# Turning keys and queries two tiles at a time, as 4-byte pairs of channels, in a fused agent-attention and maxout kernel

## The chip, the cores and the metric

The kernel runs on one core of a Trainium2 chip as one launch. The metric is the device time of one execution in microseconds: 256.32 us is the median of three runs (254.13 to 256.45). A profile of one further execution (254.07 us) gives the lines quoted here.

The core has five engines with instruction streams of their own: PE (TensorE: weight loads and matmuls, a turn of a tile among them), ACT (ScalarE), DVE (VectorE), POOL (GpSimd) and SP (SyncE, which issues the transfers here). SBUF is the working memory; PE writes to the eight banks of PSUM, and ACT and DVE copy from there.

## The reference

```python
q, k, v: (4, 12544, 128);  agents: (4, 49, 128);  w1, w2, w3: (128, 768);  w_out: (768, 128)

def sm(a, b):
    s = scale * (a @ b.transpose(0, 2, 1))
    s = s - s.max(-1, keepdims=True)
    e = np.exp(s)
    return e / (e.sum(-1, keepdims=True) + 1e-09)
a2k = sm(agents, k)
agent_v = a2k @ v
q2a = sm(q, agents)
x = (q2a @ agent_v).reshape(50176, 128)
h = np.maximum(np.maximum(x @ w1, x @ w2), x @ w3)
out = h @ w_out
```

All inputs and the output are float32. Inside, the kernel computes on bf16 values with float32 sums.

## The kernel before, in words

Tokens are handled in tiles of 128 on the partitions, with their 128 channels along the row. Each of the four batches has 98 tiles.

**Keys and values.** The 98 key tiles of a batch are 14 groups of KT = 7. Loads bring four groups at a time (28 tiles, 1792 KB for keys and as much for values; the first load of the first batch brings two groups) into five large SBUF buffers, LD. For group `kB.G` the steps are, by name: `kc` casts the keys to bf16 on POOL (into KB), `kt` turns each tile on PE so that channels are on the partitions (line L314, with the bf16 identity as the moving operand), `ke` copies the turned group from PSUM to KT on DVE (L320), `ks` multiplies each turned tile with the 49 agents of the batch (agT, L325), `kx` takes the exponent on ACT (into EK, where each tile has 64 columns, 49 of them used), `vc` casts the values (into VB, with two columns of ones behind the 128), and `kv` sums exponent times value over the batch (L339). In `kv` two tiles share a product: their 128 exponent columns are the weights and 2 x 130 value columns move, and the blocks on the diagonal are used afterwards. The seventh tile of a group is alone: 64 weight columns and 130 moving ones.

**From agents to a linear map.** After the 14 groups of a batch the sums are normalised and multiplied with the differences of the three weight matrices. Hidden units for which one of the three is largest for all agents are folded into a linear map; the others, up to 64, get a place in two small matrices. All that goes into a table G per batch. A test at the end takes a general and slow path where there are more than 64 such units; its code is not run on this data.

**Queries.** 49 query groups `s` of GT = 8 tiles: `qc` cast on POOL (QB), `qt` turn on PE (L314), `qe` copy on ACT (L568, into QT), `sc` scores, `ex` exponent on ACT (EQ), `su` and `re` sums and their reciprocals, `u`, `v`, `a`, `x` the hidden units, `p` the output products, `ov` scaling on DVE, and `st` the store of three groups at a time. In `sc` the scores of even tiles go to the lower 64 partitions of a PSUM bank and those of odd tiles to the upper 64, by two products with 64 weight columns each and 512 moving ones (L574).

**What sets the order.** The order of all steps, and the buffer and PSUM bank of each, stand in a table in the file, written out step by step; the kernel only emits it. Each engine works through its own steps in that order. A load is issued on SP when the buffer's last reader, a cast, is done. The first step, `prep` (L284), turns the agents and lays them out as agT; its turned agents stand in PSUM bank 0, which the first key turn needs next.

Of the kernel before, what the change touches and what calls it, by code (L numbers as in the profile page):

```python
# [9 lines left out]
FP32 = mybir.dt.float32  # L10
BF16 = mybir.dt.bfloat16
# [13 lines left out]
VC = C + 2  # L25
# [9 lines left out]
SLOTS = {"M": 8, "LD": 5, "QB": 3, "KB": 3, "VB": 4, "KT": 3, "QT": 3, "EQ": 8, "EK": 4, "AS": 3, "R": 3, "OS": 5}  # L35
SHAPE = {"LD": ([P, max(TK * KT, LONG), C], FP32), "QB": ([P, GT, C], BF16), "KB": ([P, KT, C], BF16), "VB": ([P, KT, VC], BF16),
         "KT": ([P, KT * C], BF16), "QT": ([P, GT, P], BF16), "EQ": ([P, 512], BF16), "EK": ([P, KT * H], BF16),
         "AS": ([P, 512], BF16), "R": ([P, 512], BF16), "OS": ([P, LONG, C], FP32)}
# [49 lines left out]


def mm(n, cols):  # L90
    t = n * max(cols / 2400 + 0.0025, 0.0253)
    return t, t + 0.235
# [18 lines left out]
def graph(plan, em):  # L111
    add = plan.add
    add("prep", PE, em.prep, (0.5, 4.0))
    for b in range(B):
        for g in range(NCH):
# [5 lines left out]
            add(f"kc{r}", POOL, em.cast("k", "kb", b, g, POOL), pool(KT * C), after=[f"kl{z}"], new=[("KB", f"kb{r}")], use=[f"k{z}"])  # L121
            add(f"kt{r}", PE, em.k_turn(r), mm(KT, 128), after=[f"kc{r}", "prep"], new=[("M", f"kT_ps{r}")], use=[f"kb{r}"])
            add(f"ke{r}", DVE, em.k_evacuate(r), (0.53, 0.72), after=[f"kt{r}"], new=[("KT", f"kT{r}")], use=[f"kT_ps{r}"])
            add(f"ks{r}", PE, em.k_scores(b, r), mm(KT, 49), after=[f"ke{r}"], new=[("M", f"s{r}")], use=[f"kT{r}"])
            add(f"kx{r}", ACT, em.k_exps(r), (0.34, 0.5), after=[f"ks{r}"], new=[("EK", f"e{r}")], use=[f"s{r}"])
            eng = ACT if b == 0 else POOL
# [72 lines left out]
class Emit:  # L199
    def __init__(self, tc, pools, io):  # L200
# [12 lines left out]
        self.sums_of = const.tile([P, KEYS + NQ * GT], FP32, name="sums_of")  # L213
        self.ag_st, self.ag_bf = self.slots["OS"][-1][:AP_, :A // 7, :], self.slots["QT"][-1][:AP_, :A // 7, :]
        nc.scalar.dma_start(self.ag_st, io["agents"].rearrange("b a c -> (b a) c").rearrange("(p j) c -> p j c", p=AP_))
# [8 lines left out]
        nc.vector.memset(self.agT, 0.0)  # L224
        self.sel = const.tile([P, 2], BF16, name="sel")
# [58 lines left out]
    def prep(self):  # L284
        nc = self.nc
        nc.vector.tensor_copy(out=self.ag_bf, in_=self.ag_st)
        t, u = self.psum[:, 0, :].bitcast(BF16), self.psum[:, 1, :]
        t = t[:, :A // 7 * 32].rearrange("c (j x) -> c j x", x=32)[:, :, :AP_]
        for j in range(A // 7):
            nc.tensor.transpose(t[:, j, :], self.ag_bf[:, j, :], self.ident[:AP_, :AP_])  # L290
        self.mul(u[:, :H], self.ones, self.earlier[:, 1:1 + H], True)
        nc.vector.tensor_copy(out=self.agT[:, :, :A].rearrange("c b (q j) -> c j b q", j=A // 7), in_=t.rearrange("c j (b q) -> c j b q", b=B))
        nc.vector.tensor_copy(out=self.slot_of, in_=u[:, :H])
# [8 lines left out]
    def cast(self, which, to, b, g, eng):  # L302
        def fn():
            z = load_of(b, g)[0]
            out, src = self.t[f"{to}{b}.{g}"][:, :, :C], self.t[f"{which}{b}.{z}"][:, (g - z) * KT:(g - z + 1) * KT, :]
            if eng == ACT:
                self.nc.scalar.activation(out, src, AF.Copy)  # L307
            else:
                self.nc.gpsimd.tensor_copy(out=out, in_=src)  # L309
        return fn  # L310
# [4 lines left out]

    def k_turn(self, r):
        return lambda: self.turn(self.t[f"kT_ps{r}"].bitcast(BF16), self.t[f"kb{r}"], KT)

    def k_evacuate(self, r):
        return lambda: self.nc.vector.tensor_copy(out=self.t[f"kT{r}"], in_=self.t[f"kT_ps{r}"].bitcast(BF16)[:, :KT * C])  # L320

    def k_scores(self, b, r):
# [5 lines left out]
    def k_exps(self, r):  # L328
        def fn():
            e, s = self.t[f"e{r}"].rearrange("p (j h) -> p j h", h=H), self.t[f"s{r}"][:, :KT * A].rearrange("p (j a) -> p j a", a=A)  # L330
            self.nc.scalar.activation(e[:, :, :A], s, AF.Exp, scale=SCALE)  # L331
# [232 lines left out]
    def q_turn(self, s):  # L564
        return lambda: self.turn(self.t[f"qT_ps.{s}"].bitcast(BF16), self.t[f"qb.{s}"], GT)

    def q_evacuate(self, s):
        return lambda: self.nc.scalar.activation(self.t[f"qT.{s}"].rearrange("p j c -> p (j c)"), self.t[f"qT_ps.{s}"].bitcast(BF16),  # L568
                                                 AF.Copy)
# [55 lines left out]

    def in_general(self):
        self.keys_in_general()
        self.queries_in_general()

    def keys_in_general(self):  # L630

        nc, ps, slots = self.nc, self.psum, self.slots
        kf, vf, kb, vb, kT, e = (slots[cls][i] for cls, i in (("LD", 0), ("LD", 1), ("KB", 0), ("VB", 0), ("KT", 0), ("EK", 0)))
        vb, e = vb[:, :, :C], e[:, :KT * A]
        eT = slots["QT"][0].rearrange("p j c -> p (j c)")[:A, :KT * P]
# [6 lines left out]
        def scores(b, g):  # L642
            nc.gpsimd.dma_start(kf[:, :KT, :], rows("k", b, g))
            nc.gpsimd.tensor_copy(out=kb, in_=kf[:, :KT, :])
# [30 lines left out]
    def queries_in_general(self):  # L675
# [13 lines left out]
        for s in range(NQ):  # L689
# [5 lines left out]
            nc.gpsimd.dma_start(self.near(s, q, GT), self.far("q", s, GT))  # L695
            nc.gpsimd.tensor_copy(out=qb, in_=q[:, half, :])
            self.turn(ps[:, 6, :].bitcast(BF16), qb, GT)
# [168 lines left out]
```

## Time and profile before

| what | before |
|---|---|
| median of three runs | 256.32 us (254.13 to 256.45) |
| profiled execution | 254.07 us, its span 252.2 us |
| PE busy | 207.6 us (82%) |
| DVE busy | 167.8 us (67%) |
| POOL busy | 151.1 us (60%) |
| ACT busy | 147.3 us (58%) |
| transfers | 104.91 MB, mean 416 GB/s |
| largest part of the chain of waits | PE, 62% |

The span runs from the first to the last instruction of the profile; the execution's own time has 1.9 us around it. An engine's busy time is the union of its instructions' times. Matmuls overlap one another, so that PE's busy time contains their run-out as well as their issue; where a step from one matmul to the next is wanted, it is worked out from the start times and the length of a merged group.

### The profile page before, as it was taken

What the parts mean: (1) busy time and instruction counts of PE and PEld (TensorE: products, weight loads), DVE (VectorE), ACT (ScalarE), POOL (GpSimd) and SP (SyncE); (2) the same over time, 40 slices, a digit from 0 to 9 for tenths busy, and PEclk for the clock granted to TensorE, in tenths of its full rate; (3) what the DMA queues carried; (4) which work ended last, traced back from release to release, by engine and by line L of the source; (5) the groups of instructions that cost most, each with busy time, mean ns of one, the idle gap of its engine ahead of it and who ended that gap; (6) DMA issues with size and microseconds to landing.
All of it is one profiled execution on the core that took longest, in us unless ns stands there. A gap on an engine that the chain in (4) does not pass through costs nothing.

```text
span 252.2 us, 6372 instructions
## 1 busy us (share of the span) xinstructions
PE 207.6 (82%) x2509; PEld 149.2 (59%) x2509; DVE 167.8 (67%) x357; ACT 147.3 (58%) x240; POOL 151.1 (60%) x171
## 2 busy tenths in 40 slices
PE   0693787759999979989898789998988989999910
PEld 0472654738686657776766567765665656676600
DVE  7342512684686689685857886585758899888940
ACT  2445257217585859285756674666566787777620
POOL 2251751896979476979691599695774444439100
PEclk9999568698999999999999999999999999999985
DMA  6999999999999999999999999999999999999994
GB/s 252 437 425 427 431 428 429 429 422 430 429 422 427 426 433 426 427 425 428 421 431 434 422 434 421 429 430 419 431 426 427 425 424 424 428 424 424 429 417 169
DMA packets 11071, 104.91 MB, mean 416 GB/s; under 512 B 1150, under 2 KB 2174, under 8 KB 3866
## 3 DMA queue, kind: packets, MB, share of 16 engines
q1 hardware_dynamic: 10992, 104.34, 97.9%
q8 instruction: 21, 0.34, 0.5%
q10 hardware_dynamic: 42, 0.10, 0.2%
q14 instruction: 16, 0.13, 0.1%
HBM read 78.74 MB, written 25.69 MB: 414 GB/s over the span
## 4 chain that ended last, share of the span: by engine, by line
PE 62%; DVE 15%; ACT 10%; DMA 5%; issue 4%; POOL 1%; ACTq 0%; DVEq 0%; POOLq 0%
PE psum L282 46%; PE psum L314 15%; DMA LD<-in_k_dram 5%; ACT QT L568 4%; DVE OS L619 3%; ACT EQ L580 2%; DVE KT L320 2%; ACT VB L307 1%; DVE gap L432 1%; DVE R L603 1%; ACT EK L331 1%; POOL KB L309 1%; DVE cand L431 1%; ACT AS L600 1%; DVE open L435 1%
## 5 line engine op out<-in xcount | busy, mean ns | idle before, releaser
L309 POOL CAST KB<-LD 128x896 bf16<-128x896 f32 x56 | 52.5, 969 | 43.7 <-DMA LD<-in_k_dram 26.2
L562 POOL CAST QB<-LD 128x1024 bf16<-128x1024 f32 x49 | 49.8, 1046 | 24.2 <-DMA LD<-in_q_dram 12.2
L619 DVE TENSOR_TENSOR OS<-psum,sums_of 128x512 f32<-128x512 f32 x97 | 61.1, 678 | 4.7 <-PE psum L282 4.5
L568 ACT ACTIVATE QT<-psum 128x1024 bf16<-128x1024 bf16 x49 | 50.3, 1026 | 18.4 <-PE psum L314 17.8
L320 DVE COPY KT<-psum 128x896 bf16<-128x896 bf16 x56 | 34.3, 620 | 24.7 <-PE psum L314 21.3
L282 PE MATMUL psum<-VB,EK 128*128 128x260 bf16 x224 | 40.3, 282 | 4.6 <-ACT VB L307 3.0
L331 ACT ACTIVATE EK<-psum 128x343 bf16<-128x343 f32 x56 | 25.7, 467 | 24.8 <-PE psum L282 14.9
L600 ACT ACTIVATE AS<-psum 128x512 bf16<-128x512 f32 x49 | 29.1, 597 | 17.9 <-PE psum L282 16.1
L314 PE MATMUL psum<-ident,KB 128*128 128x128 bf16 x392 | 35.4, 240 | 4.7 <-POOL KB L309 3.5
L603 DVE TENSOR_TENSOR R<-psum,AS 128x512 bf16<-128x512 f32 x49 | 32.7, 679 | 9.4 <-PE psum L282 4.3
L309 POOL CAST VB<-LD 128x896 bf16<-128x896 f32 x42 | 38.5, 957 | 0.3 <-DMA LD<-in_v_dram 0.3
L580 ACT ACTIVATE EQ<-psum 128x512 bf16<-128x512 f32 x49 | 29.3, 598 | 13.4 <-PE psum L282 12.7
L282 PEld LDWEIGHTS <-EK 128*128 128x128 bf16 x224 | 20.5, 103 | 24.6 <-issue 17.3
L314 PEld LDWEIGHTS <-KB 128*128 128x128 bf16 x392 | 27.5, 108 | 9.0 <-POOL KB L309 4.8
L282 PEld LDWEIGHTS <-EQ 128*128 128x128 bf16 x392 | 25.9, 97 | 10.6 <-ACT EQ L580 5.7
L282 PE MATMUL psum<-EQ,G 128*128 128x512 bf16 (+1 forms) x104 | 31.3, 366 | 0.4 <-DVE OS L619 0.2
L314 PE MATMUL psum<-ident,QB 128*128 128x128 bf16 x392 | 30.6, 222 | 0.1
L282 PE MATMUL psum<-G,R 128*128 128x256 bf16 x196 | 29.4, 273 | 1.3 <-DVE R L603 1.2
L282 PE MATMUL psum<-G,EQ 128*128 128x256 bf16 x196 | 29.4, 272 | 0.0
L314 PEld LDWEIGHTS <-QB 128*128 128x128 bf16 x392 | 23.4, 99 | 7.3 <-issue 5.9
L282 PE MATMUL psum<-QT,agT 128*64 128x512 bf16 (+1 forms) x104 | 20.1, 384 | 5.8 <-ACT QT L568 5.7
L282 PE MATMUL psum<-agT,KT 128*128 128x49 bf16 x392 | 20.7, 191 | 2.4 <-DVE KT L320 2.2
(97 smaller groups left out, 178.5 us busy)
## 6 DMA issues: line engine op xcount, KB each, us to landing
LD<-in_q_dram SPq DMA_DIRECT2D x16, 1536.0 KB, 16.2
out_dram<-OS SPq DMA_DIRECT2D x15, 1536.0 KB, 19.7
LD<-in_k_dram SPq DMA_DIRECT2D x12, 1792.0 KB, 14.3
LD<-in_v_dram SPq DMA_DIRECT2D x12, 1792.0 KB, 15.8
LD<-in_k_dram SPq DMA_DIRECT2D x4, 896.0 KB, 14.3
LD<-in_v_dram SPq DMA_DIRECT2D x4, 896.0 KB, 12.7
LD<-in_moe_w_dram SPq DMA_DIRECT2D x3, 384.0 KB, 12.9
out_dram<-OS SPq DMA_DIRECT2D x2, 512.0 KB, 11.1
```

The source lines that it names most:

```text
L282: self.nc.tensor.matmul(out, w, x, start=start, stop=True, skip_group_check=True)
L307: self.nc.scalar.activation(out, src, AF.Copy)
L309: self.nc.gpsimd.tensor_copy(out=out, in_=src)
L314: self.nc.tensor.transpose(t[:, j * P:(j + 1) * P], src[:, j, :], self.ident)
L320: return lambda: self.nc.vector.tensor_copy(out=self.t[f"kT{r}"], in_=self.t[f"kT_ps{r}"].bitcast(BF16)[:, :KT * C])
L331: self.nc.scalar.activation(e[:, :, :A], s, AF.Exp, scale=SCALE)
L562: return lambda: self.nc.gpsimd.tensor_copy(out=self.t[f"qb.{s}"], in_=self.half("q", s))
L568: return lambda: self.nc.scalar.activation(self.t[f"qT.{s}"].rearrange("p j c -> p (j c)"), self.t[f"qT_ps.{s}"].bitcast(BF16), AF.Copy)
L580: return lambda: self.nc.scalar.activation(self.t[f"e.{s}"], self.t[f"qs.{s}"], AF.Exp, scale=SCALE)
L600: return lambda: self.nc.scalar.activation(self.t[f"a.{s}"], self.t[f"u.{s}"], AF.Relu)
L603: return lambda: self.nc.vector.tensor_tensor(out=self.t[f"r.{s}"], in0=self.t[f"v.{s}"], in1=self.t[f"a.{s}"], op=ALU.max)
L619: self.nc.vector.tensor_tensor(out=out, in0=src, in1=rc.unsqueeze(2).to_broadcast([P, 4, C]), op=ALU.mult)
```

## The change

Two neighbouring tiles of bf16 values are 256 values in a row of SBUF. Seen as float32 they are 128 elements of 4 bytes, each a pair of neighbouring channels. One turn of such a block, with a float32 identity, moves both tiles: partition 64 h + i then holds the pair of channels 2i and 2i + 1 of tile h, one pair per token. So four turns do for eight tiles.

The even channels (parity x = 0) are every second bf16 element of the turned block, the odd ones the rest. The agents are laid out to match, in agP: for each parity, tile h of the pair has its own 64 rows and its own columns, with zeros elsewhere. A product over one parity gives half of the score of both tiles at once; the products of the two parities are summed in PSUM. For keys the weights are a parity of the turned block (every second element) and 2 x 49 agent columns move. For queries the copy from PSUM on ACT sorts the parities apart, and two full products of 128 weight columns and 512 moving ones write all 128 partitions of the bank.

Groups must have an even number of tiles, so key groups alternate between 8 and 6; a load of four groups is still 28 tiles. The table of the order is the same word for word, and so are all transfers. In `prep` the agents' cast, turns and layout are made in more pieces: two casts for one, 14 turns for 7, four copies for one.

```diff
+def tiles_of(g):
+    z = g // 2 * 2 * KT + g % 2 * (KT + 1)
+    return z, KT - 1 if g % 2 else KT + 1
...
-        self.agT = const.tile([P, B, H], BF16, name="agT")
+        self.agP = const.tile([P, 2, B, 2, H], BF16, name="agP")
+        self.ident_of_pairs = const.tile([P, P], FP32, name="ident_of_pairs")
+        nc.vector.tensor_copy(out=self.ident_of_pairs, in_=self.ident)
...
     def prep(self):
-        nc.vector.tensor_copy(out=self.ag_bf, in_=self.ag_st)
+        for h in range(2):
+            nc.vector.tensor_copy(out=self.ag_bf[:, :, :, h, :], in_=self.ag_st.rearrange("p j (i x) -> p j x i", x=2))
...
-        nc.vector.tensor_copy(out=self.agT[:, :, :A].rearrange("c b (q j) -> c j b q", j=A // 7), in_=t.rearrange("c j (b q) -> c j b q", b=B))
+        for h in range(2):
+            r = slice(h * H, (h + 1) * H)
+            for x in range(2):
+                nc.vector.tensor_copy(out=self.agP[r, x, :, h, :A].rearrange("c b (q j) -> c j b q", j=A // 7),
+                                      in_=t[r, x, :, :].rearrange("c j (b q) -> c j b q", b=B))
...
+    def turn_pairs(self, t, src, n):
+        two = src.rearrange("p j c -> p (j c)").bitcast(FP32)
+        for i in range(n // 2):
+            self.nc.tensor.transpose(t[:, i * P:(i + 1) * P], two[:, i * P:(i + 1) * P], self.ident_of_pairs)
...
     def k_scores(self, b, g, r):
-            for j in range(KT):
-                self.mul(self.t[f"s{r}"][:, j * A:(j + 1) * A], self.t[f"kT{r}"][:, j * P:(j + 1) * P], self.agT[:, b, :A], j == 0)
+            kT = self.t[f"kT{r}"].rearrange("p (i n x) -> p i n x", n=P, x=2)
+            for i in range(tiles_of(g)[1] // 2):
+                for x in range(2):
+                    self.mul(self.t[f"s{r}"][:, 2 * i * A:2 * (i + 1) * A], kT[:, i, :, x], self.agP[:, x, b, :, :A], i == 0 and x == 0)
...
     def values(self, b, g):
-            for j in range(0, KT, 2):
-                n = min(2, KT - j)
-                self.mul(acc[:n * H, :n * VC], e[:, j * H:(j + n) * H], vb[:, j:j + n, :].rearrange("p j c -> p (j c)"), g == 0 and j == 0)
+            for j in range(0, tiles_of(g)[1], 2):
+                self.mul(acc[:, :2 * VC], e[:, j * H:(j + 2) * H], vb[:, j:j + 2, :].rearrange("p j c -> p (j c)"), g == 0 and j == 0)
...
     def q_evacuate(self, s):
-        return lambda: self.nc.scalar.activation(self.t[f"qT.{s}"].rearrange("p j c -> p (j c)"), self.t[f"qT_ps.{s}"].bitcast(BF16),
-                                                 AF.Copy)
+        return lambda: self.nc.scalar.activation(self.t[f"qT.{s}"].rearrange("p (x i) n -> p x (i n)", x=2),
+                                                 self.t[f"qT_ps.{s}"].bitcast(BF16).rearrange("p (n x) -> p x n", x=2), AF.Copy)

     def scores(self, s, out, qT):
         for i, (b, _, n, jj, pairs) in enumerate(parts_of(s)):
-            for h in range(2):
-                self.mul(out[h * H:(h + 1) * H, jj * P:(jj + pairs) * P], self.agT[:, b, :], qT[:, h::2, :][:, jj:jj + pairs, :], i == 0)
+            for x in range(2):
+                self.mul(out[:, jj * P:(jj + pairs) * P], self.agP[:, x, b, :, :].rearrange("p h a -> p (h a)"),
+                         qT[:, x * GT // 2 + jj:x * GT // 2 + jj + pairs, :].rearrange("p i n -> p (i n)"), i == 0 and x == 0)
```

What stands on an engine changes at three places on which the prediction rests. The first is PE at the end of the first group's weighted values, `kv0.0`, and the start of the second group's scores, `ks0.1`. EK and KT are buffers of weights, VB and agT (agP) what moves; the size is that of the output. Before:

```order
L282 LDWEIGHTS EK_94
L282 MATMUL psum<-VB_76,EK_94 128x260
L282 LDWEIGHTS EK_94
L282 MATMUL psum<-VB_76,EK_94 64x130
L282 LDWEIGHTS KT_81
L282 MATMUL psum<-agT,KT_81 128x49
```

And after the change:

```order
L291 LDWEIGHTS EK_94
L291 MATMUL psum<-VB_76,EK_94 128x260
L291 LDWEIGHTS EK_94
L291 MATMUL psum<-VB_76,EK_94 128x260
L291 LDWEIGHTS KT_81
L291 MATMUL psum<-agP,KT_81 128x98
```

The product on half of the array is gone, and a score product has 98 columns where it had 49.

The second is PE at the scores of the first query group, `sc.0`, ahead of which stands the last linear product of the first batch, `py0`. Before:

```order
L282 LDWEIGHTS pick
L282 MATMUL psum<-wo_bf,pick 64x128
L282 LDWEIGHTS agT
L282 MATMUL psum<-QT_83,agT 64x512
L282 LDWEIGHTS agT
L282 MATMUL psum<-QT_83,agT 64x512
```

And after:

```order
L291 LDWEIGHTS pick
L291 MATMUL psum<-wo_bf,pick 64x128
L291 LDWEIGHTS agP
L291 MATMUL psum<-QT_83,agP 128x512
L291 LDWEIGHTS agP
L291 MATMUL psum<-QT_83,agP 128x512
```

Two products on 64 partitions each have become two on all 128.

The third is DVE at the start, in `prep` and the first two copies of turned keys. OS and QT are borrowed as staging for the agents. Before:

```order
L286 CAST QT_85<-OS_108 28x896
L292 COPY agT<-psum 128x7x4x7
L293 COPY slot_of<-psum 128x64
L320 COPY KT_80<-psum 128x896
L320 COPY KT_81<-psum 128x896
```

And after:

```order
L296 CAST OS_108<-OS_108 28x14x64 x2
L306 COPY agP<-psum 64x7x4x7 x4
L308 COPY slot_of<-psum 128x64
L344 COPY KT_80<-psum 128x1024
L344 COPY KT_81<-psum 128x768
```

Ahead of the first key copy there are three more copies and one more cast, and the key copies alternate in size.

More of the change, by code (lines that the diff above doesn't have):

```diff
@@ L121, in graph @@
             add(f"kc{r}", POOL, em.cast("k", "kb", b, g, POOL), pool(KT * C), after=[f"kl{z}"], new=[("KB", f"kb{r}")], use=[f"k{z}"])
[L122 to L125, printed above, removed]
+            add(f"kt{r}", PE, em.k_turn(g, r), mm(KT, 128), after=[f"kc{r}", "prep"], new=[("M", f"kT_ps{r}")], use=[f"kb{r}"])
+            add(f"ke{r}", DVE, em.k_evacuate(g, r), (0.53, 0.72), after=[f"kt{r}"], new=[("KT", f"kT{r}")], use=[f"kT_ps{r}"])
+            add(f"ks{r}", PE, em.k_scores(b, g, r), mm(KT, 49), after=[f"ke{r}"], new=[("M", f"s{r}")], use=[f"kT{r}"])
+            add(f"kx{r}", ACT, em.k_exps(g, r), (0.34, 0.5), after=[f"ks{r}"], new=[("EK", f"e{r}")], use=[f"s{r}"])
             eng = ACT if b == 0 else POOL
@@ L222, in __init__ @@
             nc.vector.memset(v[:, :, C:], 1.0)
[L223 to L224 removed]
+        self.agP = const.tile([P, 2, B, 2, H], BF16, name="agP")
+        nc.vector.memset(self.agP, 0.0)
+        self.ident_of_pairs = const.tile([P, P], FP32, name="ident_of_pairs")
+        nc.vector.tensor_copy(out=self.ident_of_pairs, in_=self.ident)
         self.sel = const.tile([P, 2], BF16, name="sel")
@@ L304, in fn @@
             z = load_of(b, g)[0]
-            out, src = self.t[f"{to}{b}.{g}"][:, :, :C], self.t[f"{which}{b}.{z}"][:, (g - z) * KT:(g - z + 1) * KT, :]
+            first, n = tiles_of(g)
+            out, src = self.t[f"{to}{b}.{g}"][:, :n, :C], self.t[f"{which}{b}.{z}"][:, first - z * KT:first - z * KT + n, :]
             if eng == ACT:
@@ L626, in in_general @@
     def in_general(self):
+        self.agT = self.slots["EQ"][-1][:, :B * H].rearrange("p (b h) -> p b h", b=B)
+        for x in range(2):
+            r = slice(x * H, (x + 1) * H)
+            self.nc.vector.tensor_copy(out=self.agT[r, :, :], in_=self.agP[r, x, :, x, :])
         self.keys_in_general()
@@ L643, in scores @@
             nc.gpsimd.dma_start(kf[:, :KT, :], rows("k", b, g))
-            nc.gpsimd.tensor_copy(out=kb, in_=kf[:, :KT, :])
+            nc.gpsimd.tensor_copy(out=kb.rearrange("p j (x i) -> p j x i", x=2), in_=kf[:, :KT, :].rearrange("p j (i x) -> p j x i", x=2))
             self.turn(ps[:, 0, :].bitcast(BF16), kb, KT)
@@ L695, in queries_in_general @@
             nc.gpsimd.dma_start(self.near(s, q, GT), self.far("q", s, GT))
-            nc.gpsimd.tensor_copy(out=qb, in_=q[:, half, :])
+            nc.gpsimd.tensor_copy(out=qb.rearrange("p j (x i) -> p j x i", x=2), in_=q[:, half, :].rearrange("p j (i x) -> p j x i", x=2))
             self.turn(ps[:, 6, :].bitcast(BF16), qb, GT)
```

38 lines of the change are left out of this document (22 added, 16 removed).

## The prediction

> **What bounds the kernel now.** I read the page's shares and slices first, then the table by stretch, then the end of the queue of stores, and last PE's rows one by one, because PE is what the change rewrites.
>
> ```profile
> span 252.2 us, 6372 instructions
> PE 207.6 (82%) x2509; PEld 149.2 (59%) x2509; DVE 167.8 (67%) x357; ACT 147.3 (58%) x240; POOL 151.1 (60%) x171
> DMA packets 11071, 104.91 MB, mean 416 GB/s; under 512 B 1150, under 2 KB 2174, under 8 KB 3866
> ...
> 0.00:6.00 6.00, 0.00 (x0) 0.00 (x0) 4.83 (x29) 1.28 (x1) 1.20 (x9) 1.00 0.68 243
> 6.00:12.00 6.00, 4.11 (x40) 2.93 (x40) 2.28 (x5) 2.58 (x4) 1.75 (x2) 1.00 1.03 441
> ...
> 60.00:200.00 140.00, 130.07 (x1655) 94.61 (x1653) 102.18 (x207) 90.45 (x151) 101.57 (x112) 1.00 1.01 427
> 200.00:240.00 40.00, 37.35 (x423) 25.19 (x420) 35.37 (x76) 30.55 (x47) 19.31 (x21) 1.00 1.01 425
> 240.00:246.00 6.00, 0.77 (x5) 0.41 (x5) 2.52 (x10) 1.14 (x4) 0.00 (x0) 0.80 1.01 418
> 246.00:252.00 6.00, 0.00 (x0) 0.00 (x0) 0.00 (x0) 0.00 (x0) 0.00 (x0) 0.50 0.44 169
> ```
>
> A stretch row gives PE, PEld, DVE, ACT and POOL busy time with counts, then the granted clock, the DMA engines' share and GB/s. The DMA share is 1.0 from 6 us to 246 us. The bytes alone need 104.91 MB / 427 GB/s = 245.7 us. The first six microseconds lose 6 x (427 - 243) / 427 = 2.6 us and the last six lose 6 x (427 - 169) / 427 = 3.6 us; together 251.9 of the 252.2. So the kernel is bound by its transfers, although the chain of waits runs mostly through PE. The change leaves every transfer, its size and its order alone.
>
> PE is second: idle for 9.9 us between 60 and 200 and for 2.65 us between 200 and 240. Its work can grow before it decides, but not far. How far is told by the queue:
>
> ```profile
> LD<-in_k_dram SPq DMA_DIRECT2D x12, 1792.0 KB, 14.3
> 240.33 0.33 SPq L553 DMA_DIRECT2D out_dram<-OS  x1
> 242.77 0.33 SPq L553 DMA_DIRECT2D out_dram<-OS  x1
> ```
>
> A key load of 1792 KB (1.835 MB) needs 4.3 us at 427 GB/s but lands 14.3 us after its issue: some 10 us of other transfers are queued ahead of it. The last store is issued at 242.77, and the engines are full until 246. Compute may therefore end about 3.2 us later before the engines run dry at the end. If compute ended earlier, the 169 x 6 = 1.0 MB of the last six microseconds could at best go at full rate, 2.4 us; and from 251 to 252.2 nothing but completion is left.
>
> **The change part by part.** The rows of PE that carry the terms (start, time of the merged group, count):
>
> ```profile
> 223.84 0.62 PE L314 MATMUL psum<-ident,QB 128*128 128x128 bf16 x8
> L314 PE MATMUL psum<-ident,QB 128*128 128x128 bf16 x392 | 30.6, 222 | 0.1
> L314 PEld LDWEIGHTS <-QB 128*128 128x128 bf16 x392 | 23.4, 99 | 7.3 <-issue 5.9 <-POOL KB L309 0.2
> 88.38 0.53 PEld L282 LDWEIGHTS psum<-fold,cand 128*128 128x128 f32 x4
> L282 PEld LDWEIGHTS psum<-fold,cand x16: 186/192/333, 44.9 to 195.7; 128*128 128x128 f32 x16
> ...
> 112.95 0.67 PE L282 MATMUL psum<-VB,EK 128*128 128x260 bf16 x4
> 113.55 0.35 PE L282 MATMUL psum<-agT,KT 128*128 128x49 bf16 x7
> 113.83 0.41 PE L282 MATMUL psum<-QT,agT 128*64 128x512 bf16 x2
> 114.17 0.68 PE L282 MATMUL psum<-VB,EK 128*128 128x260 bf16 x4
> 114.97 0.59 PE L282 MATMUL psum<-EQ,G 128*128 128x512 bf16 x2
> 115.40 0.67 PE L282 MATMUL psum<-VB,EK 128*128 128x260 bf16 x4
> ...
> L282 PE MATMUL psum<-agT,KT x392: 183/183/248, 9.1 to 189.1; 128*128 128x49 bf16 x196
> L282 PE MATMUL psum<-G,R 128*128 128x256 bf16 x196 | 29.4, 273 | 1.3 <-DVE R L603 1.2
> 88.05 0.60 PE L282 MATMUL psum<-G,R 128*128 128x256 bf16 x4
> ```
>
> *Turns.* Eight turns take 0.62 us of which the last one's own 222 ns is mostly run-out: a step of (620 - 222) / 7 = 57 ns, so 784 turns cost 44.7 us. Afterwards there are 392 turns of 4-byte elements. No 4-byte turn is in the trace; the nearest rows are the 4-byte weight loads of the small product with fold: (530 - 192) / 3 = 113 ns from one to the next, with 49 columns moved. The low bound is the 2-byte step, 57 ns (22.3 us, a gain of 22). The high bound comes from the same rows: line L282 is called twice for each of four batches, 8 calls, and the trace holds 16, so a 4-byte product is made in two passes; two passes per turn are 226 ns (88.6 us, a loss of 44). I take one load at 113 ns, since the built program holds one load and one matmul for each 4-byte turn, and two of each for a product with fold: 44.3 us, change 0.
>
> The Trainium skill, page "TensorE: Matmul & The Clock Gate", section "Terms", says that weight loads and matmuls on this chip have a transpose mode that is four times faster for 4-byte data. If that made a 4-byte turn as quick as a 2-byte one, the sum would be that of the low bound; no row here shows it. The same page, section "Weight-path perf modes", leaves 4-byte data out of the fast weight load; by that rule the load of 113 ns stays, and the trace's 192 ns against 99 ns for 2-byte loads agrees.
>
> *Weighted values (line L339).* A group of seven tiles takes three products of 260 columns and a half one of 130 on 64 array columns; from 112.95 to the next start at 113.55 it is 600 ns. The product of G and R shows the step of 256 columns, (600 - 273) / 3 = 109 ns, and the turn that of 128, 57: 0.41 ns a column, so 111 for 260. Now an eight-tile group takes 4 x 111 = 444 and a six-tile group 333, in the mean 388. That the half product costs 600 - 333 = 267 ns instead of some 57 shows a wait around it, which goes with it: 56 x 0.212 = 11.9 us less PE.
>
> *Key scores.* Seven products of 49 columns have a step of (350 - 183) / 6 = 28 ns; the same number now moves 98 columns, between 28 and 57 ns, by 0.41 ns a column about 44. 56 x 7 x 16 ns = 6.3 us more. The strided weights may at worst reach 57: 11.4 us.
>
> *Query scores.* The two products on half the array run side by side: 113.83 to 114.17 is 340 ns for both, and the group before ends its issue at 113.55 + 0.19 = 113.74, so 90 ns go in the switch. Two full products in sequence take what L282's pair from EQ and G takes, 114.97 to 115.40, 430 ns. Change 0, at worst 49 x 0.09 = 4.4 us.
>
> PE's sum: 0 - 11.9 + 6.3 + 0 = -6 us, bounds -28 and +48, all of it in the stretch before 200 that the transfers cover; after 200 there are no keys and the sum is 0, so the last store is issued where it is now. Cost on the time: nothing. If that cover were gone, -6 us would be seen.
>
> *Copies and casts.* POOL, DVE and ACT handle the same columns in two sizes (1024 and 768 for 896); a mean of a straight line is the same. The query copy on ACT now reads every second 2-byte element:
>
> ```profile
> L568 ACT ACTIVATE QT<-psum 128x1024 bf16<-128x1024 bf16 x49 | 50.3, 1026 | 18.4 <-PE psum L314 17.8 <-PE psum L282 0.4
> L580 ACT ACTIVATE EQ<-psum 128x512 bf16<-128x512 f32 x49 | 29.3, 598 | 13.4 <-PE psum L282 12.7 <-DVE R L603 0.5
> L331 ACT ACTIVATE EK<-psum 128x343 bf16<-128x343 f32 x56 | 25.7, 467 | 24.8 <-PE psum L282 14.9 <-issue 8.9 <-ACT cand L413 0.6
> ```
>
> Reads with a 4-byte step are there as float reads: (598 - 467) / 169 = 0.775 ns a column, which for 1024 gives 995 ns, against 1026 now. So the step is free by the rows; the upper bound is a doubling, 49 x 1.03 = 50 us of ACT. I take 0.
>
> The Trainium skill, page "SBUF — State Buffer", section "Door 1: The DMA port swizzle", calls PSUM lines 8 bytes long and says that non-contiguous PSUM patterns slow matmuls much. It speaks of matmuls; were it to hold for this copy, the doubling would be the estimate, and the float rows speak against that.
>
> *The start.* DVE prepares the agents before the first turn, whose PSUM bank the agents' turns hold:
>
> ```profile
> LD<-in_k_dram SPq DMA_DIRECT2D x4, 896.0 KB, 14.3
> LD<-in_moe_w_dram SPq DMA_DIRECT2D x3, 384.0 KB, 12.9
> 0.72 0.39 SPq L299 DMA_DIRECT2D LD<-in_k_dram  x1
> ...
> 5.46 0.61 DVE L286 CAST QT<-OS 28x896 bf16<-28x896 f32 x1
> 6.53 0.91 DVE L292 COPY agT<-psum 128x196 bf16<-128x196 bf16 x1 [0.45 <-PE psum L290]
> 7.10 0.38 DVE L293 COPY slot_of<-psum 128x64 f32<-128x64 f32 x1
> ...
> 2.87 4.36 SPq L346 DMA_DIRECT2D LD<-in_moe_w_dram  x2
> 10.95 0.33 SPq L299 DMA_DIRECT2D LD<-in_k_dram  x1
> ```
>
> One copy becomes four of as many columns (step 7.10 - 6.53 = 0.57): 1.7 to 2.7 us; the cast in two, the larger clears, the float identity and seven more small turns add about 1 us by the rows of their kind. So the first scores, the value cast behind them on ACT and the load at 10.95 that waits for it slip by about 3 us, with the weight load behind it on SP. Issued by 7.2 us are two loads of 896 KB, two of 1792 and two of 384, 6.29 MB; by 12 us 6 x 243 + 6 x 441 = 4.1 MB have moved, so 2.2 MB or 5.1 us are left: dry at 17.1. The 6 x 243 = 1.46 MB of the first row are 3.4 us at full rate, so bytes began to flow at 2.6, some 2 us after the first issue at 0.72; 10.95 + 3 + 2 = 16 is in time, by a microsecond. Cost 0; without the cover up to 2 us.
>
> The whole sum is 0 on the profiled execution: its span of 252.2 and 1.9 around it, 254.07. That execution is among the quick ones: the runs go from 254.13 to 256.45 with the median at 256.32 and the mean at 255.6. As the middle of such a draw I take 255.6.
>
> **The rivals.** *A 4-byte turn takes the time of two passes, 226 ns (slower).* For: the only 4-byte products in the trace take it, 16 rows for 8 calls. Against: the built program has one pass per turn, so that one pass would have to last twice as long as the load that the trace shows. Of 49 queries 34 lie between 60 and 200 and 14 after (the query copies, counted by stretch), of 56 key groups 38 between 60 and 200:
>
> ```profile
> 60.00:200.00 140.00, 34.85 (x34) 1.00 1.01 427
> 200.00:240.00 40.00, 14.38 (x14) 1.00 1.01 425
> 60.00:200.00 140.00, 23.36 (x38) 1.00 1.01 427
> ```
>
> A query gains 4 x 113 = 0.45 us, a key group 3.5 x 113 - 212 + 112 = 295 ns. From 60 to 200: 34 x 0.45 + 38 x 0.295 - 9.9 idle = 16.6 us; after: 14 x 0.45 - 2.65 idle - 3.2 queued = 0.5. About 255.6 + 17 = 272. It decides once PE grows by more than its 12.5 us of idle time and the 3.2.
>
> *ACT's strided read doubles (slower).* ACT's 30.55 of 40 us after 200 becomes 30.55 + 14.4 = 45: 5 us too much, less 3.2 queued, 257.5; with waits in fixed order up to 261.
>
> *Turns as quick as 2-byte ones (faster).* PE loses 28 us, 14 x 4 x 56 ns = 3.1 us of it after 200. The last store goes out 3 us sooner, but the bytes hold the end: at most the 2.4 us above, 253.2, half a step from 1%.
>
> *The four copies at the start starve the queue.* Two microseconds, 257.6, still no change.
>
> **How the numbers follow.** About 1% (2.6 us) is what a measurement of this kernel tells from no change. Transfers bind and nothing moves: 0.65, with the starved start in it. Quick turns: 0.17, of which half ends beyond 1%; with runs that fall low by chance, faster 0.13. Turns of 226 ns: 0.11; ACT: 0.07, five sevenths of it beyond 1%; with high draws of the first case slower 0.17. Same 0.70. The range goes from 252.6, the quick turns at their limit with a low draw, to 260.5, most of the ACT case; what lies outside is mainly the turns of 226 ns.
>
> **What would show it.** Right: DMA share 1.0 from 6 to 246 us again, near 104.9 MB; 392 turns with a step near 113 ns; values groups without the gap before the half product (388 ns in the mean); query scores at 430 ns; the query copy at 1026 ns. Wrong: 784 rows of 4-byte turns or a step over 150 ns, a DMA share under 0.95 in the middle, a query copy near 2 us, or a hole in the transfers at 17 us.

## The result, and the profile after

The changed kernel takes 256.07 us in the median of its runs (254.76 to 260.65), the kernel before on the same chip 254.30; the ratio is 1.0061, with a 95% interval of 1.0040 to 1.0081. So the change costs 1.8 us by the medians; the ratio, which is of the means without one slow run of each kernel, gives 1.6 us (1.0 to 2.1). That is less than the 1% that was called "no change", and more than the measurement is uncertain by. The profiled execution took 256.14 us, of which 254.2 are its span.

The shares of the page, and then the table by stretch (PE, PEld, DVE, ACT and POOL busy time with counts, the granted clock, the share of the DMA engines, GB/s), both of the changed kernel:

```profile
span 254.2 us, 5584 instructions
PE 205.6 (81%) x2096; PEld 158.9 (62%) x2096; DVE 173.1 (68%) x362; ACT 146.3 (58%) x240; POOL 150.8 (59%) x171
DMA packets 11069, 104.86 MB, mean 412 GB/s; under 512 B 1151, under 2 KB 2175, under 8 KB 3867
```

```profile
12.00:18.00 6.00, 4.50 (x27) 3.33 (x28) 1.52 (x4) 1.65 (x3) 2.80 (x3) 1.00 1.01 413
18.00:24.00 6.00, 5.29 (x47) 4.45 (x45) 3.48 (x5) 2.52 (x5) 0.83 (x1) 1.00 0.96 387
24.00:60.00 36.00, 23.97 (x245) 19.29 (x242) 16.45 (x29) 16.85 (x30) 22.11 (x24) 0.84 1.01 420
60.00:200.00 140.00, 130.30 (x1378) 102.02 (x1378) 101.42 (x203) 89.49 (x150) 101.81 (x112) 0.99 1.01 428
```

The three stretches of the kernel before that answer to the first three:

```profile
12.00:18.00 6.00, 5.46 (x55) 4.35 (x56) 2.50 (x4) 2.18 (x5) 3.58 (x4) 1.00 1.02 430
18.00:24.00 6.00, 3.32 (x29) 1.82 (x27) 2.11 (x2) 4.38 (x6) 0.00 (x0) 1.00 0.99 418
24.00:60.00 36.00, 26.56 (x311) 19.88 (x312) 16.04 (x29) 14.74 (x27) 23.68 (x25) 0.72 1.01 428
```

From 60 to 200 us the two kernels move their bytes at the same rate, 428 and 427 GB/s. The loss lies ahead of that. The bytes that were not moved, put as time at 427 GB/s, are (430 - 413) x 6 / 427 = 0.24 us from 12 to 18, (418 - 387) x 6 / 427 = 0.44 from 18 to 24, and (428 - 420) x 36 / 427 = 0.67 from 24 to 60: 1.35 of the 2.0 us by which the span of the profiled execution grew. The loss isn't made good later, since the transfers are busy up to 246 us. The other 0.65 us are not followed here. Some lie in the first six microseconds, (243 - 227) x 6 / 427 = 0.22, and some in the last two, where about one of the sixteen DMA engines is still at work (a share of 0.06):

```profile
252.00:254.00 2.00, 0.00 (x0) 0.00 (x0) 0.00 (x0) 0.00 (x0) 0.00 (x0) 0.50 0.06 23
```

Between 18 and 30 us the transfers run short more than once. Single microseconds of the changed kernel, with the same columns:

```profile
18.00:19.00 1.00, 1.00 (x7) 0.98 (x5) 0.00 (x0) 0.00 (x0) 0.00 (x0) 1.00 0.78 302
27.00:28.00 1.00, 0.03 (x1) 0.03 (x2) 0.00 (x0) 0.92 (x1) 0.80 (x1) 1.00 0.85 345
29.00:30.00 1.00, 1.00 (x5) 0.64 (x4) 1.00 (x2) 0.00 (x0) 0.68 (x1) 0.50 0.67 273
```

A single microsecond is a coarse measure, though: the kernel before has one too, at 15 us, with a share of 0.76 and 317 GB/s, made good by 1.29 and 536 at 17, and the microsecond ahead of the last row above has a share of 1.51. Over three microseconds at a time the shortfall stays: the changed kernel moves 378 GB/s from 18 to 21 us and 358 from 27 to 30, the kernel before 416 and 448.

What leaves late around these places are the loads of keys and values. The timeline of the changed kernel's start (start, length, engine, line, operation, count, and in brackets the idle time before it and who ended it):

```profile
6.02 1.06 DVE L296 CAST OS<-OS 28x896 bf16<-28x896 f32 x1
7.02 1.06 DVE L296 CAST OS<-OS 28x896 bf16<-28x896 f32 x1
8.72 3.38 DVE L306 COPY agP<-psum 64x196 bf16<-64x196 bf16 x4 [0.64 <-PE psum L301]
12.13 0.23 DVE L308 COPY slot_of<-psum 128x64 f32<-128x64 f32 x1
12.24 1.73 PE L336 MATMUL psum<-ident_of_pairs,KB 128*128 128x128 f32 x7 [3.39 <-DVE agP L306]
15.38 0.83 ACT L323 ACTIVATE VB<-LD 128x768 bf16<-128x768 f32 x1
16.24 0.33 SPq L314 DMA_DIRECT2D LD<-in_k_dram  x1
```

The first turn of the keys waits for DVE's four copies and starts at 12.24. The first scores, their exponentials and, at 15.38, the second value cast on ACT follow, and that cast sets free the buffer into which SP loads at 16.24. In the kernel before the same load leaves at 10.95. The slip is 5.3 us, and by the rows of the same queue the next four loads of keys and values leave 4.2, 5.5, 4.2 and 2.3 us later than before.

The engines' own work came out as it was costed. These are rows of the changed kernel's PE, one for each kind of product, and the groups whose mean gives the last product's own time:

```profile
100.76 0.52 PE L291 MATMUL psum<-agP,KT 128*128 128x98 bf16 x8
102.08 0.59 PE L291 MATMUL psum<-QT,agP 128*128 128x512 bf16 x2
103.70 0.61 PE L291 MATMUL psum<-VB,EK 128*128 128x260 bf16 x4
109.01 0.60 PE L336 MATMUL psum<-ident_of_pairs,QB 128*128 128x128 f32 x4
L336 PE MATMUL psum<-ident_of_pairs,QB 128*128 128x128 f32 x196 | 30.0, 276 | 0.2 <-ACT AS L628 0.2
L291 PE MATMUL psum<-agP,KT 128*128 128x98 bf16 x392 | 28.8, 217 | 3.1 <-DVE KT L344 2.8
L291 PE MATMUL psum<-VB,EK 128*128 128x260 bf16 x196 | 31.4, 279 | 6.8 <-ACT VB L323 5.3
L291 PE MATMUL psum<-QT,agP 128*128 128x512 bf16 x96 | 28.5, 378 | 5.2 <-ACT QT L595 5.0 <-DVE cand L458 0.2
L595 ACT ACTIVATE QT<-psum 128x1024 bf16<-128x1024 bf16 x49 | 50.1, 1023 | 16.4 <-PE psum L336 15.9
```

A turn steps by (600 - 276) / 3 = 108 ns, a key score by (520 - 217) / 7 = 43, a value product by (610 - 279) / 3 = 110, a query score by 590 - 378 = 212. The page counts 392 turns with 4-byte elements (196 of keys and 196 of queries), each with one load.

### The profile page after: what moved, and what is told of

Read it like the earlier page. It is cut to its first block, busy times and chain, and to the rows that moved or that the text cites. A ratio compares the mean times of both kernels' runs of the same rounds, so it can differ in the third digit from the quotient of the medians.

```text
span 254.2 us, 5584 instructions
## 1 busy us (share of the span) xinstructions
PE 205.6 (81%) x2096; PEld 158.9 (62%) x2096; DVE 173.1 (68%) x362; ACT 146.3 (58%) x240; POOL 150.8 (59%) x171
## 2 busy tenths in 40 slices
DMA packets 11069, 104.86 MB, mean 412 GB/s; under 512 B 1151, under 2 KB 2175, under 8 KB 3867
## 4 chain that ended last, share of the span: by engine, by line
PE 58%; DVE 9%; ACT 8%; issue 3%; DMA 2%; ACTq 0%; DVEq 0%
PE psum L291 46%; PE psum L336 13%; ACT QT L595 3%; DMA out_dram<-OS 2%; DVE OS L647 2%; ACT EQ L608 2%; DVE gap L459 1%; DVE KT L344 1%; ACT VB L323 1%; ACT AS L628 1%; ACT EK L359 1%; DVE cand L458 1%; DVE R L631 1%; DVE pick L481 1%; DVE cand L411 0%
## 5 line engine op out<-in xcount | busy, mean ns | idle before, releaser
L325 POOL CAST KB<-LD 128x1024 bf16<-128x1024 f32 (+1 forms) x56 | 52.4, 964 | 46.2 <-PE psum L336 23.6
L595 ACT ACTIVATE QT<-psum 128x1024 bf16<-128x1024 bf16 x49 | 50.1, 1023 | 16.4 <-PE psum L336 15.9
L344 DVE COPY KT<-psum 128x1024 bf16<-128x1024 bf16 (+1 forms) x56 | 34.0, 619 | 25.7 <-PE psum L336 24.1
L359 ACT ACTIVATE EK<-psum 128x392 bf16<-128x392 f32 (+1 forms) x56 | 25.8, 465 | 28.3 <-PE psum L291 19.5
L325 POOL CAST VB<-LD 128x1024 bf16<-128x1024 f32 (+1 forms) x42 | 38.4, 954 | 0.4 <-DMA LD<-in_v_dram 0.4
L336 PE MATMUL psum<-ident_of_pairs,KB 128*128 128x128 f32 x196 | 35.0, 307 | 3.8 <-DVE agP L306 3.4
L291 PE MATMUL psum<-QT,agP 128*128 128x512 bf16 (+1 forms) x104 | 29.1, 366 | 5.4 <-ACT QT L595 5.2
L291 PE MATMUL psum<-agP,KT 128*128 128x98 bf16 x392 | 28.8, 217 | 3.1 <-DVE KT L344 2.8
L336 PEld LDWEIGHTS psum<-ident_of_pairs,KB 128*128 128x128 f32 x196 | 25.7, 158 | 7.4 <-issue 5.0
L336 PE MATMUL psum<-ident_of_pairs,QB 128*128 128x128 f32 x196 | 30.0, 276 | 0.2 <-ACT AS L628 0.2
L291 PEld LDWEIGHTS <-KT 128*128 128x128 bf16 x392 | 23.8, 103 | 9.4 <-DVE KT L344 7.3
```

Of the source, the lines that this page charges most:

```text
L291: self.nc.tensor.matmul(out, w, x, start=start, stop=True, skip_group_check=True)
L336: self.nc.tensor.transpose(t[:, i * P:(i + 1) * P], two[:, i * P:(i + 1) * P], self.ident_of_pairs)
L344: self.nc.vector.tensor_copy(out=self.t[f"kT{r}"][:, :n], in_=self.t[f"kT_ps{r}"].bitcast(BF16)[:, :n])
L359: self.nc.scalar.activation(e[:, :n, :A], s, AF.Exp, scale=SCALE)
```

## The experiments

Two theories were set against each other. By the first, the start costs the time: DVE's longer preparation of the agents holds back the first loads, the transfers run dry, and the rest of the change is free. By the second, the rest costs it: the query scores in sequence, and the other steps of PE, end later, and the last store leaves late. There is a row for it: the last store of the changed kernel leaves at 245.35, 2.6 us later than before.

```profile
245.35 0.33 SPq L580 DMA_DIRECT2D out_dram<-OS  x1
```

**A late start without the change.** The kernel before, whose DVE does the cast of the agents four times and the copy of their turns seven times.

```diff
-        nc.vector.tensor_copy(out=self.ag_bf, in_=self.ag_st)
+        for _ in range(4):
+            nc.vector.tensor_copy(out=self.ag_bf, in_=self.ag_st)
...
-        nc.vector.tensor_copy(out=self.agT[...], in_=t...)
+        for _ in range(7):
+            nc.vector.tensor_copy(out=self.agT[...], in_=t...)
```

> The kernel before, with the agents' cast on DVE made four times and the copy of the turned agents seven times, so that the first key turn comes about 5 us later (near 12 us, as after the change). Nothing else differs. Start theory (the later start lets the transfer engines run dry between 17 and 37 us, and those bytes are never made up): 1.5 to 2 us slower than before, near 256 against 254.3. Query-score theory (two score products in sequence lengthen each query's chain, and the last store leaves 2.6 us later): no change, 254.3.

It took 259.59 us against 254.24, a ratio of 1.0212 (1.0195 to 1.0228), more than the 256 that were expected. The delay came out longer than was meant, since a copy that is repeated steps by 0.94 us and not by the 0.57 to the next operation; the load leaves at 19.77. The kernel's timeline and its table by stretch:

```profile
5.46 3.80 DVE L287 CAST QT<-OS 28x896 bf16<-28x896 f32 x4
9.72 6.54 DVE L294 COPY agT<-psum 128x196 bf16<-128x196 bf16 x7 [0.46 <-PE psum L291]
19.77 0.33 SPq L301 DMA_DIRECT2D LD<-in_k_dram  x1
...
12.00:18.00 6.00, 1.68 (x16) 1.44 (x16) 4.80 (x7) 0.00 (x0) 1.57 (x2) 1.00 0.93 389
18.00:24.00 6.00, 4.88 (x44) 3.17 (x45) 1.51 (x3) 1.76 (x3) 2.08 (x3) 1.00 0.53 196
24.00:60.00 36.00, 25.50 (x295) 18.16 (x293) 17.45 (x28) 19.34 (x32) 17.49 (x20) 0.86 0.99 407
```

By the same working as above the transfers lose 0.58 + 3.12 + 1.77 = 5.5 us, and the kernel took 5.35 longer. With no turn, score or value product changed, a late start alone costs what the transfers lose in it.

**Half of that.** The kernel before with two casts and four copies.

```diff
+        for _ in range(2):
+            nc.vector.tensor_copy(out=self.ag_bf, in_=self.ag_st)
...
+        for _ in range(4):
+            nc.vector.tensor_copy(out=self.agT[...], in_=t...)
```

> As the run with the start delayed by 5 us, but the cast twice and the copy four times: about 2.3 us later. Start theory with the cover worked out in the prediction (a load that waits for the start may leave about 4 us later before the engines run dry at 17 us): within 0.4 us of before. If the loss grows in a line with the delay instead, about 0.8 us slower. Query-score theory: no change.

```profile
15.03 0.33 SPq L301 DMA_DIRECT2D LD<-in_k_dram  x1
```

The load is 4.1 us late, where 2.3 were meant, and the time is 254.89, a ratio of 1.0039 (1.0018 to 1.0061). That is more than the 0.4 us that were expected, but only 0.65 us of the 4.1 reach the end by the medians, 1.0 by the ratio. There is slack at the start; the table further down shows where it ends.

**The changed kernel with a lighter start.** The clears of avT, G, wall, ub, vb and rd go to POOL, and one of the two casts and two of the four copies to ACT.

```diff
-            nc.vector.memset(t, 0.0)
+            nc.gpsimd.memset(t, 0.0)
...
+                if h:
+                    nc.scalar.activation(out, src, AF.Copy)
+                else:
+                    nc.vector.tensor_copy(out=out, in_=src)
```

> The changed kernel with its start made short: the clears of avT, G, wall, ub, vb and rd on POOL instead of DVE, one of the two agents' casts and two of the four copies on ACT. The first key turn should come near 7 to 8 us, as before the change. Start theory: the loss goes, 254.3 to 254.8 against 254.3 of before. Query-score theory: still 1.5 to 2 us slower than before, near 256.

The timeline of its start:

```profile
5.91 1.26 DVE L225 CAST fold<-ident 64x49 f32<-64x49 bf16 x2
6.09 1.81 POOL L328 CAST KB<-LD 128x1024 bf16<-128x1024 f32 x2
7.19 0.80 DVE L233 CAST ident_of_pairs<-ident 128x128 f32<-128x128 bf16 x1
9.67 1.69 ACT L308 ACTIVATE agP<-psum 64x196 bf16<-64x196 bf16 x2 [3.97 <-DVE slot_of L311]
15.53 0.33 SPq L317 DMA_DIRECT2D LD<-in_k_dram  x1
```

Little was saved, 0.7 us at the load: ACT's copies did not run beside DVE's but after them, and the two small casts on DVE took longer than in the changed kernel. It took 255.03 us, a ratio of 1.0046 (1.0029 to 1.0063), where 254.3 to 254.8 were expected. The load is between the two, and so is the time; the run is in line with the first theory but is too small a step to decide.

**The changed kernel with a heavier start.** Each of the four copies is made twice.

```diff
-            for x in range(2):
+            for x in (0, 0, 1, 1):
                 nc.vector.tensor_copy(out=self.agP[...], in_=t[...])
```

> The changed kernel with each of the four copies of the turned agents made twice: the first key turn about 3.3 us later again, near 15.5 us. Start theory: 2 to 3.3 us slower than the changed kernel, 258 to 259.5, since no cover is left. Query-score theory: as the changed kernel, 256.

```profile
20.06 0.33 SPq L314 DMA_DIRECT2D LD<-in_k_dram  x1
...
12.00:18.00 6.00, 1.79 (x8) 1.43 (x9) 4.87 (x8) 0.00 (x0) 1.94 (x3) 1.00 0.91 380
18.00:24.00 6.00, 4.74 (x30) 3.52 (x31) 1.24 (x3) 1.65 (x3) 1.79 (x2) 1.00 0.48 165
24.00:60.00 36.00, 25.39 (x242) 20.47 (x242) 16.47 (x29) 19.23 (x32) 18.98 (x20) 0.86 1.00 416
```

259.65 us, a ratio of 1.0226 (1.0204 to 1.0248). The load leaves 3.8 us later than in the changed kernel, and the time is 3.6 us longer: behind the slack a microsecond costs almost a microsecond. The transfers lose 0.70 + 3.56 + 1.01 = 5.3 us against the kernel before, and the time 5.4. It is also level with the first experiment, in which the load leaves at the same time and nothing else is changed.

**The whole change with a quick start.** The agents are loaded as two blocks of 98 rows, so that four turns do for 14 and two copies with runs of 49 elements for the four scattered ones; the clear of G is put off to a later place on DVE.

```diff
-CAPACITY, AP_ = 64, B * 7
+CAPACITY, AP_ = 64, 2 * A
...
-            for j in range(A // 7):
+            for j in range(2):
...
-            for x in range(2):
-                nc.vector.tensor_copy(out=self.agP[r, x, :, h, :A].rearrange("c b (q j) -> c j b q", j=A // 7), ...)
+            nc.vector.tensor_copy(out=self.agP[r, :, :, h, :A], in_=t[r, :, :].rearrange("c x (b a) -> c x b a", b=B))
```

> The changed kernel with a quick start: the agents are loaded as 2 x 98 rows, so that four turns do for 14 and two copies with runs of 49 for four scattered ones, and the clears of G stand later. The load that waits for the start should leave at 11 to 12 us (before 10.95, with the change 16.24). Start theory: the whole loss goes, 254.0 to 254.5 against 254.2 of before, and no faster, since the transfers bind. If something else of the change costs time as well (the query scores in sequence): 254.8 or more.

```profile
8.44 0.74 DVE L305 COPY agP<-psum 64x392 bf16<-64x392 bf16 x2
13.33 0.33 SPq L312 DMA_DIRECT2D LD<-in_k_dram  x1
...
12.00:18.00 6.00, 4.74 (x32) 3.70 (x32) 1.20 (x2) 1.70 (x4) 3.63 (x4) 1.00 1.01 423
18.00:24.00 6.00, 3.84 (x41) 2.70 (x39) 4.16 (x7) 5.79 (x9) 1.25 (x2) 1.00 1.02 434
24.00:60.00 36.00, 25.01 (x258) 20.46 (x260) 16.37 (x29) 15.01 (x27) 22.47 (x24) 0.79 1.01 428
```

254.32 us against 254.23, a ratio of 1.0003 (0.9991 to 1.0015). The load leaves later than the 11 to 12 us that were expected, but still in time: the dips are gone and with them the loss, although all of the turns, scores and value products are those of the change. The second theory falls here: nothing but the start costs more than the 0.4 us that the interval leaves. Its last store leaves at 243.9, a microsecond later than before, and that is free.

**The control.** The same start in the kernel before.

```diff
-CAPACITY, AP_ = 64, B * 7
+CAPACITY, AP_ = 64, 2 * A
...
-        for j in range(A // 7):
-            nc.tensor.transpose(t[:, j, :], self.ag_bf[:, j, :], self.ident[:AP_, :AP_])
+        for j in range(2):
+            nc.tensor.transpose(t[:, j * AP_:(j + 1) * AP_], self.ag_bf[:, j, :], self.ident[:AP_, :AP_])
```

> The kernel before with the same quick start, the control: its load that waits for the start leaves before 10.95 us. Start theory: no change (254.2), since that load was in time already. If an earlier start were worth time by itself, it would be 0.5 us or more faster.

254.00 us, a ratio of 0.9994 (0.9969 to 1.0019). The load leaves at 11.87 here, later than without the edit and not earlier as expected, and the time doesn't move. Whether a still earlier load would gain anything is therefore not shown. The quick start brings nothing of its own, and what it gave to the changed kernel is the loss that it took back.

The six kernels and the two given ones line up by one number, whichever kernel it is:

| kernel | first gated load leaves, us | time, us | ratio to before |
|---|---|---|---|
| before | 10.95 | 254.24 | |
| before, quick start | 11.87 | 254.00 | 0.9994 |
| changed, quick start | 13.33 | 254.32 | 1.0003 |
| before, two casts and four copies | 15.03 | 254.89 | 1.0039 |
| changed, lighter start | 15.53 | 255.03 | 1.0046 |
| changed | 16.24 | 256.07 | 1.0061 |
| before, four casts and seven copies | 19.77 | 259.59 | 1.0212 |
| changed, heavier start | 20.06 | 259.65 | 1.0226 |

The load's time is that of each kernel's one profiled execution, the other columns are of all its runs; the profiled execution of the lighter start took 254.22 us, no longer than the kernel before. Taking the time lost off the load's time tells where the slack ends: 15.03 - 0.65 = 14.4, then 14.7, 14.5, 14.4 and 14.7 for the last five rows. So up to some 14.5 us a late load is free, and behind that a microsecond costs a microsecond, whether the change is in the kernel or not. A loss in a straight line from 10.95 on doesn't fit: 2.4 us late costs 0.1 us, 4.1 costs 0.65 and 9.1 costs 5.4.

**Without most of the stores.** Two more runs ask what the change would be worth if transfers did not cover it: the kernel before, and the changed one with the quick start, both without the thirteen stores of the first 39 query groups, 20.4 MB of 104.9.

```diff
     def store(self, s, n):
+        if s < TG * 13:
+            return lambda: None
```

> The kernel before with the 13 stores of query groups 0 to 38 left out (20.4 MB less; those rows of the output are not written), so that the transfers need about 198 us at 427 GB/s and no longer bind. This shows what compute alone takes; PE's 207.6 us of busy time and the waits between engines then decide: 225 to 245 us.

> The changed kernel with the quick start and the same 13 stores left out. If PE's gain of about 6 us is real and hidden by the transfers: 2 to 6 us less than the kernel before without these stores. If the change gains nothing in compute, or loses (the longer chain of the query scores): the same or more.

The kernel before took 251.86 us, a ratio of 0.9921 (0.9900 to 0.9941), where 225 to 245 us were expected; the changed one 252.86, 0.9932 (0.9908 to 0.9955). With four runs each the two can't be told apart. Their stretches, of the kernel before first, each followed by the queue's row for the last six query loads:

```profile
60.00:200.00 140.00, 128.54 (x1630) 94.13 (x1646) 102.41 (x208) 90.29 (x151) 102.96 (x114) 1.00 0.95 390
200.00:240.00 40.00, 35.97 (x406) 24.72 (x409) 35.67 (x75) 29.46 (x45) 17.23 (x19) 1.00 0.23 93
174.53 17.02 SPq L550 DMA_DIRECT2D LD<-in_q_dram  x6
```

```profile
60.00:200.00 140.00, 128.69 (x1346) 102.27 (x1366) 102.41 (x206) 89.96 (x149) 101.67 (x112) 0.99 0.95 389
200.00:240.00 40.00, 37.00 (x360) 26.91 (x364) 35.33 (x75) 29.92 (x46) 18.88 (x21) 1.00 0.20 79
176.53 16.61 SPq L577 DMA_DIRECT2D LD<-in_q_dram  x6
```

The question is answered for the stretch after 200 alone. There the transfers stand nearly still (share 0.23 and 0.20), PE is busy for 36 and 37 of 40 us, and the change gains nothing. Up to 200 the cover was only thinned, to a share of 0.95, so the 6 us that PE should save among the keys stay unseen. The last query loads leave 2.0 us later in the changed kernel, but its first gated load already left 2.4 us later (13.31 against 10.96).

## Why the prediction came out as it did

The forecast was that nothing moves; the kernel became 1.6 to 1.8 us slower. The forecast of 255.6 us lies near the 256.07 measured, but partly by chance: it started from a middle of 255.6 for the kernel before, which then ran at 254.3 beside the changed one.

**The step that failed is the start, in three places.** The path was seen rightly: the agents' preparation on DVE, the first scores, the value cast, the load. Its size was not.

First, "the load at 10.95 slips by about 3 us": it slipped by 5.3. The four copies take 3.41 us from the first to the next operation (8.72 to 12.13) where the one took 0.57, 2.8 more against the 1.7 to 2.7 allowed; 0.57 was the step to another, shorter operation, and a copy behind its like steps by 0.85. The casts, clears and turns, put down at "about 1 us", cost 2.2: each of the two casts writes all 896 columns (28x14x64 x2 in the order ahead of the prediction) and takes 1.06 us, where "the cast in two" had counted them as halves of one of 0.61; together they add 1.45, the first starts 0.56 later (6.02 against 5.46), and 14 turns instead of seven 0.18. The first key turn follows 0.3 sooner behind the last of these than it did, and the first two groups, of eight and six tiles, take 4.0 us from there to the load (12.24 to 16.24) where those of seven took 3.5. With 5.3 in place of 3 the prediction's own sum reads 10.95 + 5.3 + 2 = 18.2 against "dry at 17.1", and the first shortfall stands behind 18 us. By that sum a load was in time up to 17.1 - 2 = 15.1 us; the runs put it at some 14.5, so that this part was off by half a microsecond only.

The second place is that only the first load was followed. The stretch from 18 to 21 us alone is worth (416 - 378) x 3 / 427 = 0.27 us of the 1.35. The shortfall goes on to 30 us, and the loads behind the first left 2.3 to 5.5 us late as well; that these are its cause there is read from the order of times and was not tried by itself.

The third is the choice itself: the margin was one microsecond, the upper price, "without the cover up to 2 us", was worked out and is near what came, and the term was still set to 0.

**The rival that held** is the starved start. It was given two microseconds, and 1.6 to 1.8 were measured. It was kept as a part of the first case because it stayed under 1%. A hole in the transfers at 17 us was on the list of what would show the forecast wrong; it came, behind 18 us and again from 27 to 30. A DMA share of 1.0 from 6 to 246 us, a sign of being right, failed with 0.96 from 18 to 24 us. A share under 0.95 in the middle did not come (1.01 from 60 to 200).

**What held.** Transfers bind: 104.86 MB, a share of 1.0 but for that one stretch, and what the transfers lost at the start came out in the time (5.5 and 5.35 us, 5.3 and 5.4 in the two runs with the latest loads). *Turns*: 113 ns were taken and 108 measured, with one load and one matmul each. So the two rivals on the turns, 57 ns and 226 ns, are out: 4 bytes step by 108 ns where 2 bytes step by 57. With the first goes the reading that the four-fold transpose mode of the Trainium skill (page "TensorE: Matmul & The Clock Gate", section "Terms") makes a 4-byte turn as quick as a 2-byte one. That the load is what they step by is in line with the 113 ns of the 4-byte loads, but it is not shown: four products that move 256 2-byte columns, as many bytes as a turn moves, step by 109 ns, and no run tells the two apart. The rule of the same page's section "Weight-path perf modes", which leaves 4-byte data out of the fast load, agrees with the step. *Values*: 111 ns a product, measured 110, and the gap before the half product is gone. *Key scores*: about 44 ns, measured 43. *Query scores*: 430 ns for two, measured 424. *The query copy*: 1023 ns with a 4-byte step against 1026; the doubling did not come, so that the slowing of non-contiguous PSUM patterns, which the Trainium skill states for matmuls (page "SBUF — State Buffer", section "Door 1: The DMA port swizzle"), is not seen on this copy.

**What was wrong but hidden.** "The last store is issued where it is now": it left 2.6 us later. Most of it goes with the late start and not with the scores: in the kernel before with two casts and four copies it is 1.8 us late (244.54), without any change to the scores, and in the changed kernel with the quick start 1.1, which costs nothing. **What stays open:** whether the 6 us that PE saves among the keys would be seen without cover. PE's busy time fell by 2 us only (207.6 to 205.6), though a busy sum of overlapping records is no measure of its steps; and no run freed that stretch of its transfers. Open too is whether the weight load or the moving side sets the step of a 4-byte turn.

## What to carry to other kernels

In a kernel whose transfers are busy from end to end, what a change does to the first loads decides, even where it was made for the middle: find the first load that waits for a buffer, follow who sets that buffer free, and work out how late it may leave before the engines run dry. Price an added small operation by how it steps behind its like, not by the step to whatever comes next, and treat a margin of a microsecond that rests on three estimates as none. Two 2-byte tiles turned as one 4-byte tile halved the turns and left their time where it was, because each then stepped by 108 ns in place of 57.

## What had not been expected of the hardware

**A fifth of the bytes less, and hardly less time.** Taking away 20.4 MB of stores, 47.8 us of transfers at 427 GB/s, made the kernel before only 2.4 us shorter. What is left, the loads up to some 192 us (the last six leave from 174.5 to 191.5) and PE behind them, takes 251.9 us. That isn't compute alone, since up to 200 us the DMA share was still 0.95. But what had looked like a kernel bound by its bytes alone has a second bound, of loads and then compute, that lies only about 1% below. The 3.2 us by which, in the prediction's estimate, compute could end later are of the same size.

**Scattered copies are dear.** In the changed kernel a copy of 196 2-byte elements out of PSUM, written in a scattered order, takes 0.85 us, 4.3 ns an element. With runs of 49 the 392 elements of the quick start's copies take 0.74 / 2 = 0.37 us each, 0.9 ns an element, less than a quarter.

**A busy POOL went with slow casts on DVE.** This is seen together and was not tried by itself. The two casts into fold took 1.26 us in the kernel with the lighter start, beside POOL's casts of the first keys, and 0.32 in the kernel before with its cast and copy repeated, where no POOL cast ran yet; the one into the float identity took 0.80 there and 0.23 in the changed kernel, ahead of POOL's casts. The rows of the timelines of these two, in that order:

```profile
4.37 0.32 DVE L218 CAST fold<-ident 64x49 f32<-64x49 bf16 x2
5.04 0.23 DVE L233 CAST ident_of_pairs<-ident 128x128 f32<-128x128 bf16 x1
```

It isn't so for every cast: the agents' casts took 1.06 us in the changed kernel, where the second of them lay beside POOL's, and 1.07 us in the lighter start, where POOL made clears and no cast yet. These casts read every second value. The agents' cast of the kernel before reads them in order: it took 0.61 us where it began ahead of POOL's casts, and in the run with two casts the two took 1.88 us, so that the second, beside POOL's, took about twice the first. The order of reading may be what sets the two kinds apart.
